# A Strassen-Winograd kernel: two quarter operands of a second-level step made as one full-width operand, and one more product split a second time

## The chip, the cores and the metric

One core of a Trainium2 chip runs one program. The metric is the device time in microseconds (us) of one execution; of several runs the median is given. TensorE (PE) multiplies, VectorE (DVE) and ScalarE (ACT) prepare operands and take results out of PSUM, GpSimd (POOL) and SyncE (SP) issue transfers.

## The reference, cut to what matters

```python
# x: 2048 x 1024, fp32; dft matrices 1024^2 and 2048^2; w1: 1024 x 3584; w2: 3584 x 1024
a, b = x @ hid_re.T, x @ hid_im.T                 # stage x
y = seq_re @ a - seq_im @ b                       # stage C ("sequence"), K = 4096
h = relu(x @ w1 + b1) ** 2                        # stage h: part 0 (2048 columns), part 1 (1536)
o = h @ w2 + b2                                   # stage o ("output"), K = 3584
g = sigmoid((x * gate_w).sum(-1, keepdims=True))
out = g * y + (1 - g) * o
```

All of it is fp32 and nearly all of the work is in four large matrix products.

## The kernel before, in words

Each number is split into a high and a low part that TensorE takes at its fast rate: `hi` is the value rounded by ScalarE (`ACTIVATE hi<-raw`), `lo` is what VectorE leaves over (`TENSOR_TENSOR lo<-raw,hi`). A product of two operands is then three matmuls: hi by hi, hi by lo, lo by hi (`Group.run`).

A stage is a Winograd variant of Strassen's scheme: seven products of half-size blocks in place of eight, with block sums S1 to S4 of the left side and T1 to T4 of the right (`FACTORS` says which product takes which block or sum). `seven` walks through the products in the order of a tuple (1, 2, 5, 6, 3, 7, 4). A product runs either whole (`direct`) or is split once more into seven (`twice`). Which are split stands in tables: `TWICE_X`, `TWICE_C`, `TWICE_O` and, for the two parts of stage h, `TWICE_H`. Before, part 0 of h splits all seven, part 1 splits all but product 7.

There are two shapes of stage. `wide` (stages x and h) has a short inner dimension. A whole product is 8 steps of `rows` * 6 matmuls, a split one 7 steps; `rows` is 4, and 3 in part 1 of h, so that a step there is 18 matmuls. In a split product the seven steps run in the order 5, 1, 3, 6, 2, 7, 4; steps 1, 6, 7 and 4 form a chain that goes on adding in the same PSUM tiles, which are read out behind every step, before the next step of the chain may write there. Steps 7 and 4 follow each other directly. `tall` (stages C and o) has a long inner dimension and splits for 2 * k of its blocks, k from the table; there the left operands of the second level are 256 wide. Such an operand has its high and its low part in one tile, `both`. Blocks (0,1) and (1,1) of the second level (steps 2 and 4) are the two 256-wide halves of one block `base[1, q]` of the first level, and before each of them is made as an operand of its own: two ACT instructions and two DVE instructions of 128x512.

The order of the work is not written down. The kernel records its operations, and `plan` lays them out: a list scheduler with due times counted back from an unbroken run of matmuls, 55 tile slots that are handed out in the order of need, and four PSUM tiles. `emit` then writes that one order, so every instruction of an engine has the same source line (L1512 in the profile) and groups are told apart by tile names: `raw` loaded, `sum` a block sum, `h`, `u`, `y`, `o` results, `ps` PSUM. Tables choose between equal ways of one thing: `MINUS` makes a low part by an ACT copy and an adding transfer of POOL in place of DVE; `LAND`, `LAND2` and `MADE` make block sums by adding transfers; `LOW` and `HIGH` keep finished low and high parts in HBM and fetch them again; `RELU` lets DVE do the bias and the relu of a quarter of h.

Of the kernel before, what the change touches and what calls it, by code (L numbers as in the profile page):

```python
# [22 lines left out]
FIRST_C, FIRST_O = {1: 6, 2: 5, 3: 5, 6: 3, 7: 6}, {6: 3, 7: 3}  # L23
# [2 lines left out]
LAND_X, LAND_C, LAND_H, LAND_O = {"T1": 4}, {"T1": 16, "T3": 4, "T4": 15}, ({"T1": 4, "T3": 2}, {"T3": 4}), {"T1": 8, "T3": 2, "T4": 11}
# [2 lines left out]
ADD_O = range(13)
GATE, ROWS = (-30, 2), (24, 24)  # L30
OLD_X, OLD_H = (2, 3, 4), ((3, 4, 2, 6), (3,))
# [1 line left out]
LOW, HIGH = ({1: 125, 2: 35, 3: 119, 4: 32, 5: 7, 6: 3, 7: 6}, {1: 4, 2: 125, 3: 119, 4: 1, 5: 127, 6: 112, 7: 1}), ({5: 64, 6: 8, 7: 65}, {2: 2, 3: 35, 4: 42, 6: 64, 7: 18})
# [1 line left out]
LAND2_X, LAND2_C, LAND2_H, LAND2_O = {}, {1: {"T3": 3}, 2: {"T1": 4, "T3": 3}, 3: {"T1": 3, "T3": 3}, 4: {"T1": 3, "T3": 1}, 6: {"T1": 1}, 7: {"T1": 1}}, ({2: ("T1",), 5: ("T1",), 3: ("T1", "T3"), 6: ("T3",)}, {1: ("T3",), 2: ("T3",), 5: ("T3",), 3: ("T3",)}), {1: {"T1": 1}, 2: {"T1": 3, "T3": 1}, 3: {"T1": 3, "T3": 3}, 4: {"T1": 2, "T3": 3}, 5: {"T1": 2, "T3": 1}, 6: {"T1": 1}}
MADE = {"T1": 2600, "T3": 12076}
TWICE_H = (1, 2, 5, 3, 4, 6, 7), (1, 2, 5, 3, 4, 6)
# [13 lines left out]
LATE, PATIENT = 60.0, (20.0, 0)  # L51
# [1511 lines left out]
```

## Time and profile before

| what | us |
|---|---|
| median of 3 runs | 1821.21 (1816.94, 1821.21, 1821.67) |
| the profiled execution | 1817.16 |
| its span, first to last instruction | 1815.4 |
| PE busy | 1799.3 (99%) |
| DVE busy | 1713.9 (94%) |
| ACT busy | 1172.8 (65%) |
| POOL busy | 279.3 (15%) |

The span is what the profiler saw of the program, and 1.8 us of the execution lie outside it. Matmuls overlap, so that a single one lasts 0.39 us while they start 0.23 us apart; times of matmuls are therefore read from their starts. By the count of matmuls the stages lie at about 6 to 283 us (x), to 836 (C), to 1103 (h part 0), to 1308 (h part 1) and to 1800 (o).

### The profile page before, as it was taken

The page shows a single profiled execution, that of the slowest core. Times are in us where ns is not written, and L with a number is a line of the kernel's source. Part 1 is how long each engine was busy: PE and PEld are TensorE (multiplying, and loading weights), DVE is VectorE, ACT ScalarE, POOL GpSimd, SP SyncE. Part 2 cuts the span into 40 slices and gives each one's busy share as a digit, 9 for nine tenths or more (in the row PEclk, how much of TensorE's full clock was granted, in tenths as well). Part 3 has the DMA queues.
Part 4 walks back from the last instruction along what each step waited for, and adds up shares of the span by engine and source line. Part 5 has one row for each costly group of instructions (what it writes and reads, how often), then busy time and mean ns, then how long its engine had stood idle before and what let it go on. Part 6 is the DMA issues. An engine that isn't in the chain of part 4 may idle for free. (4 is left out here: it accounts for less than half of the span.)

```text
span 1815.4 us, 22435 instructions
## 1 busy us (share of the span) xinstructions
PE 1799.3 (99%) x7940; PEld 1484.2 (82%) x7940; DVE 1713.9 (94%) x1758; ACT 1172.8 (65%) x1362; POOL 279.3 (15%) x408
## 2 busy tenths in 40 slices
PE   9999999999999999999999999999999999999998
PEld 7888888888888888888888888878788888888886
DVE  8999989999999999999888999688898999999997
ACT  6465655674666564667684749968986566675662
POOL 1202112011211000211210211012121021101121
PEclk9999999999999999999999999999999999999999
DMA  9999999899999689989998889999999999879986
GB/s 349 319 395 356 397 332 317 285 258 306 256 344 304 183 293 374 283 212 351 329 360 255 283 312 310 375 385 339 321 375 249 345 207 307 292 202 339 308 237 134
DMA packets 155872, 552.68 MB, mean 304 GB/s; under 512 B 17504, under 2 KB 17776, under 8 KB 155760
## 3 DMA queue, kind: packets, MB, share of 16 engines
q1 hardware_dynamic: 96768, 345.70, 50.9%
q0 software_dynamic: 58704, 205.16, 42.3%
q8 instruction: 62, 1.02, 0.2%
q10 hardware_dynamic: 288, 0.39, 0.1%
q14 instruction: 50, 0.41, 0.1%
HBM read 397.56 MB, written 138.42 MB: 295 GB/s over the span
## 5 line engine op out<-in xcount | busy, mean ns | idle before, releaser
L1512 PE MATMUL ps<-hi,both 128*128 128x512 f32 x2072 | 640.6, 389 | 0.8 <-ACT ps L1512 0.4
L1512 PE MATMUL ps<-hi 128*128 128x512 f32 x1596 | 621.4, 390 | 4.5 <-ACT hi L1512 2.3
L1512 PE MATMUL ps<-hi,lo 128*128 128x512 f32 x1596 | 620.7, 389 | 1.6 <-DVE lo L1512 1.6
L1512 PE MATMUL ps<-lo,hi 128*128 128x512 f32 x1596 | 620.5, 389 | 0.0
L1512 ACT ACTIVATE hi<-raw 128x1024 fp32r<-128x1024 f32 (+2 forms) x412 | 419.2, 1034 | 210.2 <-PE ps L1512 72.9
L1512 PEld LDWEIGHTS ps<-hi,both 128*128 128x128 f32 x2072 | 388.7, 188 | 82.9 <-ACT ps L1512 1.4
L1512 DVE TENSOR_TENSOR lo<-raw,hi 128x1024 fp32r<-128x1024 f32 (+2 forms) x353 | 414.8, 1189 | 30.8 <-ACT hi L1512 24.1
L1512 PE MATMUL ps<-lo,both 128*128 128x512 f32 x1036 | 403.5, 389 | 0.3 <-DMA lo<-sum 0.3
L1512 PEld LDWEIGHTS ps<-hi 128*128 128x128 f32 x1596 | 299.5, 188 | 70.2 <-ACT hi L1512 3.8
L1512 PEld LDWEIGHTS ps<-hi,lo 128*128 128x128 f32 x1596 | 299.6, 188 | 64.9 <-DVE lo L1512 2.4
L1512 PEld LDWEIGHTS ps<-lo,hi 128*128 128x128 f32 x1596 | 299.5, 188 | 62.2 <-DVE lo L1512 0.4
L1512 ACT ACTIVATE hi<-sum 128x1024 fp32r<-128x1024 f32 (+1 forms) x215 | 220.8, 1034 | 137.2 <-DVE sum L1512 95.8
L1512 DVE TENSOR_TENSOR lo<-sum,hi 128x1024 fp32r<-128x1024 f32 (+1 forms) x203 | 239.7, 1190 | 14.3 <-ACT hi L1512 11.1
L1512 PEld LDWEIGHTS ps<-lo,both 128*128 128x128 f32 x1036 | 194.5, 188 | 41.6 <-DMA lo<-sum 1.1
L1512 DVE TENSOR_TENSOR raw<-raw 128x1024 f32<-128x1024 f32 (+1 forms) x164 | 193.0, 1196 | 3.7 <-DMA raw<-in_w1b 1.3
L1512 DVE TENSOR_TENSOR sum<-raw 128x1024 f32<-128x1024 f32 (+2 forms) x181 | 177.4, 986 | 6.2 <-PE ps L1512 3.3
L1512 DVE TENSOR_TENSOR sum<-raw,sum 128x1024 f32<-128x1024 f32 (+2 forms) x138 | 144.9, 1050 | 2.8 <-PE ps L1512 2.5
L1512 ACT ACTIVATE both<-sum 128x512 fp32r<-128x512 f32 x148 | 90.7, 625 | 79.4 <-DVE sum L1512 74.5
L1512 ACT ACTIVATE u<-ps 128x1024 f32<-128x1024 f32 x104 | 101.6, 979 | 29.8 <-PE ps L1512 29.5
L1512 ACT ACTIVATE both<-raw 128x512 fp32r<-128x512 f32 x111 | 68.5, 623 | 53.6 <-PE ps L1512 13.5
L1512 DVE TENSOR_TENSOR both<-sum,both 128x512 fp32r<-128x512 f32 x148 | 99.7, 683 | 0.6 <-ACT both L1512 0.5
L1512 DVE TENSOR_TENSOR u<-u,ps 128x1024 f32<-128x1024 f32 x74 | 86.4, 1178 | 7.6 <-PE ps L1512 5.9
(80 smaller groups left out, 1092.1 us busy)
## 6 DMA issues: line engine op xcount, KB each, us to landing
raw<-in_ct SPq DMA_DIRECT2D x130, 512.0 KB, 7.2
raw<-h SPq DMA_DIRECT2D x99, 512.0 KB, 7.1
raw<-in_w SPq DMA_DIRECT2D x94, 512.0 KB, 9.1
raw<-copy SPq DMA_DIRECT2D x73, 512.0 KB, 7.2
raw<-ab SPq DMA_DIRECT2D x71, 512.0 KB, 8.4
raw<-in_x SPq DMA_DIRECT2D x51, 512.0 KB, 9.1
copy<-raw POOLq DMA_DIRECT2D x46, 512.0 KB, 8.1
lo<-lo SPq DMA_DIRECT2D x46, 512.0 KB, 7.4
```

The source lines that it names most:

```text
L1512: made = getattr(real[op.engine], op.name)(*(actual(a) for a in op.args), **{k: actual(v) for k, v in op.kwargs.items()})
```

## The change

Part 1 of h now splits product 7 too. In stages C and o the operands (0,1) and (1,1) of a split product are made at once, as one 512-wide operand with a tile `hi` and a tile `lo`, and steps 2 and 4 take a half each (`Half`). A class `Twin` would do the same for S1 and S3; it is switched by bit 0 of `TWINS`, which isn't set. `RELU` now gives DVE one quarter of part 1 of h. The other tables are set anew.

```diff
-FIRST_C, FIRST_O = {1: 6, 2: 5, 3: 5, 6: 3, 7: 6}, {6: 3, 7: 3}
+FIRST_C, FIRST_O = {1: 6, 2: 5, 6: 4, 7: 6}, {6: 3, 7: 3}
...
-ADD_O = range(13)
-GATE, ROWS = (-30, 2), (24, 24)
+ADD_O = range(8)
+GATE, ROWS = (-30, 2), (20, 20)
...
-TWICE_H = (1, 2, 5, 3, 4, 6, 7), (1, 2, 5, 3, 4, 6)
+TWICE_H = (1, 2, 5, 3, 4, 6, 7), (1, 2, 5, 3, 4, 6, 7)
...
-EARLY_C, EARLY_O = 0, 65535
+EARLY_C, EARLY_O = 65535, 65535
...
-MINUS_C, MINUS_O = {2: 133124, 3: 8388624, 4: 8388613, 5: 50331652, 6: 8519745}, {1: 16, 2: 8, 3: 267264, 4: 12591136, 5: 9221, 6: 5243142, 7: 6291464}
-RELU = (), ()
+MINUS_C, MINUS_O = {2: 133124, 3: 8425522, 4: 8912905, 5: 33554436, 6: 1179713, 7: 4096}, {1: 16, 2: 8390664, 3: 410628, 4: 12595208, 5: 9221, 6: 6, 7: 6422568}
+RELU = (), (0,)
+TWINS_C, TWINS_O = 2, 2
...
+                    if block.seen and block.home == "slot" and not op.load and not block.seen[0][0].load:
+                        op.after.add(block.seen[0][0])
...
             for q in range(k):
                 again = Sums(lambda j, c, q=q: right[2 * q + j, c].of(r), SUMS_R2, True)
                 again.made.update({key: r2[q].of(key) for key in ("T1", "T2")})
+                pair = Operand(base[1, q]) if twins & 2 else None
                 for p2 in (2, 4, 3):
                     l_, r_ = FACTORS[p2]
-                    own.append((l2[q].operand(l_, 256), subtracted(p, again.operand(r_)), groups[p2],
+                    own.append((Half(pair, 256 * (p2 == 4)) if pair and p2 != 3 else l2[q].operand(l_, 256), subtracted(p, again.operand(r_)), groups[p2],
                                 [(2 * q + j, c) for j in range(2) for c in range(2)] if p2 == 3 else ()))
```

`LAND`, `LAND2`, `MADE`, `LOW`, `HIGH`, `OLD_H` and `PATIENT` change in the same manner, in their numbers only.

Three places of the instruction order follow. The first is VectorE near the beginning of stage C, in the split of product 1. Before, block `raw_2504` gives two operands:

```order
L1512 TENSOR_TENSOR sum_2995<-raw_2910,sum_2604 128x1024
L1512 TENSOR_TENSOR lo_3002<-raw_2910,hi_2981 128x1024
L1512 TENSOR_TENSOR both_2989<-raw_2504,both_2989 128x2x256
L1512 TENSOR_TENSOR both_3008<-raw_2504,both_3008 128x2x256
L1512 TENSOR_TENSOR lo_3026<-sum_2995,hi_3012 128x1024
L1512 TENSOR_TENSOR lo_3035<-raw_2644,hi_3022 128x1024
```

Now the same block, `raw_2507`, gives one:

```order
L1542 TENSOR_TENSOR sum_2996<-raw_2914,sum_2605 128x1024
L1542 TENSOR_TENSOR lo_3003<-raw_2914,hi_2981 128x1024
L1542 TENSOR_TENSOR lo_3014<-raw_2507,hi_2991 128x1024
L1542 TENSOR_TENSOR lo_3025<-sum_2996,hi_3007 128x1024
L1542 TENSOR_TENSOR lo_3034<-raw_2651,hi_3017 128x1024
```

The pair of 128x512 has become a single 128x1024, and the rows around it keep their order. ACT changes in the same way.

The second place is VectorE in product 7 of part 1 of h. Before, the results of a group, in two PSUM tiles, are added to `h` as the group ends, between operands that it makes:

```order
L1512 TENSOR_TENSOR h_10236<-h_10236,ps_10857 128x1024
L1512 TENSOR_TENSOR h_10269<-h_10269,ps_10874 128x512
L1512 TENSOR_TENSOR lo_11031<-sum_10985,hi_10998 128x2x384
L1512 TENSOR_TENSOR lo_11039<-raw_10923,hi_11027 128x1024
L1512 TENSOR_TENSOR h_10409<-h_10409,ps_10937 128x1024
L1512 TENSOR_TENSOR lo_11064<-raw_10849,hi_11046 128x2x384
L1512 TENSOR_TENSOR h_10425<-h_10425,ps_10952 128x512
```

Now they are added to `u`, behind every step:

```order
L1542 TENSOR_TENSOR u_10494<-u_10494,ps_10899 128x1024
L1542 TENSOR_TENSOR u_10506<-u_10506,ps_10924 128x512
L1542 TENSOR_TENSOR lo_11025<-sum_10992,hi_11002 128x2x384
L1542 TENSOR_TENSOR sum_11030<-raw_10793,sum_10913 128x768
L1542 TENSOR_TENSOR u_10494<-u_10494,ps_10939 128x1024
L1542 TENSOR_TENSOR u_10506<-u_10506,ps_10969 128x512
L1542 TENSOR_TENSOR raw_10941<-raw_10941,raw_10136 128x768
L1542 TENSOR_TENSOR lo_11060<-sum_11030,hi_11044 128x2x384
```

The read-outs of PSUM stand closer together, and `u` is added to `h` later.

The third place is PE in the same product, with the semaphores that an instruction waits for. Before, a group of product 7 starts in a PSUM tile that the group ahead of it does not use:

```order
L1512 MATMUL ps_10874<-hi_10867,hi_10879 128x512
L1512 MATMUL ps_10874<-lo_10882,hi_10879 128x512
L1512 MATMUL ps_10874<-hi_10867,lo_10897 128x512
L1512 MATMUL ps_10937<-hi_10885,hi_10822 128x512 [waits Activation_49]
L1512 MATMUL ps_10937<-lo_10909,hi_10822 128x512
```

Now, at the border from step 7 to step 4 of the split product, the tile is one that the step before has written, and that VectorE has to read first:

```order
L1542 MATMUL ps_10969<-lo_11000,hi_11002 128x512
L1542 MATMUL ps_10969<-hi_10984,lo_11025 128x512
L1542 MATMUL ps_10939<-hi_11034,hi_11044 128x512 [waits DVE_49,Activation_49]
L1542 MATMUL ps_10939<-lo_10954,hi_11044 128x512 [waits DMAHW4_49]
L1542 MATMUL ps_10939<-hi_11034,lo_11060 128x512
```

The first matmul of step 4 now waits for a DVE read of `ps_10939` that stands, in the DVE rows above, four rows ahead of the last low part of that step.

## Rows read from the trace of the kernel before

**Rows 1.** The page: the span, and the engines' busy time, share and instructions.

```profile
span 1815.4 us, 22435 instructions
PE 1799.3 (99%) x7940; PEld 1484.2 (82%) x7940; DVE 1713.9 (94%) x1758; ACT 1172.8 (65%) x1362; POOL 279.3 (15%) x408
```

**Rows 2.** Timeline of PE at both ends: start, duration, instruction, [idle before <-releaser].

```profile
5.96 0.73 PE L1512 MATMUL ps<-hi 128*128 128x512 f32 x2 [0.99 <-ACT hi L1512]
...
1807.14 0.39 PE L1512 MATMUL ps<-hi,lo 128*128 128x512 f32 x1
```

**Rows 3.** Groups by shape, PE, warm-up: count | busy us, mean ns | idle before.

```profile
L1512 PE MATMUL ps<-ones 128*128 128x128 bf16 x44 | 3.9, 274 | 1.1 <-DVE ones L1512 1.1
```

**Rows 4.** The chain that ended last: start, length, what, its longest piece.

```profile
1633.15 171.67 PE ps L1512 x756
```

**Rows 5.** PE's waits over the whole span: total us, times, longest.

```profile
PE ps L1512 <- ACT hi L1512: 2.3, 2, 1.3
PE ps L1512 <- DVE lo L1512: 1.6, 1, 1.6
...
PE ps L1512 <- ACT ps L1512: 0.4, 1, 0.4
```

**Rows 6.** Timeline of PE in part 1 of h, at the borders of split products.

```profile
1132.63 0.50 PE L1512 MATMUL ps<-hi 128*128 128x512 f32 x1 [0.52 <-DVE u L1512]
...
1161.12 0.39 PE L1512 MATMUL ps<-hi,lo 128*128 128x512 f32 x1
1161.55 0.47 PE L1512 MATMUL ps<-hi 128*128 128x512 f32 x1
...
1191.71 0.50 PE L1512 MATMUL ps<-hi 128*128 128x512 f32 x1 [1.27 <-DVE h L1512]
...
1249.49 0.47 PE L1512 MATMUL ps<-hi 128*128 128x512 f32 x1
...
1312.28 0.47 PE L1512 MATMUL ps<-hi 128*128 128x512 f32 x1 [1.32 <-ACT hi L1512]
```

**Rows 7.** Stretches C, h part 1, o: us, busy us (count) by engine, clock, DMA.

```profile
283.00:836.00 553.00, 552.66 (x2434) 456.21 (x2433) 544.08 (x581) 344.11 (x406) 72.31 (x93) 1.00 0.93 289
...
1103.00:1308.00 205.00, 203.08 (x891) 166.57 (x890) 169.16 (x182) 177.88 (x233) 31.95 (x51) 1.00 1.00 354
1308.00:1800.00 492.00, 489.99 (x2160) 404.83 (x2159) 479.21 (x514) 316.11 (x369) 72.54 (x90) 1.00 0.92 277
```

**Rows 8.** Groups by shape, DVE, ACT and POOL: the operations that the change touches.

```profile
L1512 ACT ACTIVATE hi<-raw 128x1024 fp32r<-128x1024 f32 x382 | 397.6, 1054 | 198.2 <-DVE raw L1512 67.0 <-PE ps L1512 66.7 <-DMA raw<-copy 10.3
L1512 DVE TENSOR_TENSOR lo<-raw,hi 128x1024 fp32r<-128x1024 f32 x323 | 388.6, 1217 | 16.8 <-ACT hi L1512 10.4 <-PE ps L1512 3.1 <-ACT h L1512 2.8
L1512 DVE TENSOR_TENSOR u<-u,ps 128x1024 f32<-128x1024 f32 x69 | 83.1, 1215 | 7.6 <-PE ps L1512 5.9 <-ACT u L1512 0.8
L1512 DVE TENSOR_TENSOR both<-raw,both 128x512 fp32r<-128x512 f32 x111 | 74.3, 682 | 0.0
L1512 ACT ACTIVATE both<-raw 128x512 fp32r<-128x512 f32 x111 | 68.5, 623 | 53.6 <-PE ps L1512 13.5 <-DVE raw L1512 12.8 <-DMA raw<-in_w 8.2
L1512 ACT ACTIVATE h<-h,b1c 128x512 f32<-128x512 f32 x97 | 65.5, 711 | 2.0 <-DVE h L1512 2.0
L1512 DVE TENSOR_TENSOR lo<-sum,hi 128x768 fp32r<-128x768 f32 x21 | 20.0, 953 | 10.5 <-ACT hi L1512 7.7 <-PE ps L1512 2.8
L1512 DVE TENSOR_SCALAR g<-g 128x1024 f32<-128x1024 f32 x2 | 1.3, 682 | 0.0
```

**Rows 9.** DMA totals in h part 1, then in its stretch 1140 to 1170.

```profile
DMA packets 21171, 72.48 MB, mean 354 GB/s; under 512 B 2385, under 2 KB 2385, under 8 KB 21158
...
DMA packets 3461, 11.83 MB, mean 394 GB/s; under 512 B 388, under 2 KB 388, under 8 KB 3457
```

**Rows 10.** The chain ahead of the matmul at 1191.71: start, length, what.

```profile
1177.91 7.27 issue
1185.20 5.32 DMA h<-h
```

More of the change, by code (lines that the diff above doesn't have):

```diff
@@ L22 @@
 TWICE_X, TWICE_C, TWICE_O = (1, 2, 5, 3, 4), {1: 4, 2: 4, 3: 4, 4: 4, 5: 3, 6: 1, 7: 1}, {1: 2, 2: 3, 3: 3, 4: 3, 5: 3, 6: 1, 7: 1}
[L23 removed]
+FIRST_C, FIRST_O = {1: 6, 2: 5, 6: 4, 7: 6}, {6: 3, 7: 3}
 WARM = 44
 FAR_TALL, FAR_WIDE = ("T2",), ()
[L26 removed]
+LAND_X, LAND_C, LAND_H, LAND_O = {"T1": 4}, {"T1": 16, "T3": 2, "T4": 15}, ({"T3": 2}, {"T3": 3}), {"T1": 9, "T3": 4, "T4": 11}
 SHARE = ("S1", "S2", "S3", "S4")
 NEAR_O = ("T1",)
[L29 to L31 removed]
+ADD_O = range(8)
+GATE, ROWS = (-30, 2), (20, 20)
+OLD_X, OLD_H = (2, 3, 4), ((3, 4, 2), (3, 6))
 SHARE2 = {1: 15, 2: 15, 3: 15, 4: 15, 5: 15, 6: 15, 7: 15}
[L33 removed]
+LOW, HIGH = ({1: 125, 2: 35, 3: 119, 4: 32, 5: 7, 6: 113, 7: 19}, {1: 4, 2: 125, 3: 127, 4: 1, 5: 127, 6: 112, 7: 9}), ({1: 1, 2: 32, 5: 64, 6: 8, 7: 73}, {3: 19, 4: 42, 6: 64, 7: 18})
 SPILL, LAND_CL = (8, 0), {"S1": 1}
[L35 to L37 removed]
+LAND2_X, LAND2_C, LAND2_H, LAND2_O = {3: ("T1",), 4: ("T1", "T3"), 5: ("T3",)}, {1: {"T3": 3}, 2: {"T1": 4, "T3": 3}, 3: {"T1": 3, "T3": 2}, 4: {"T1": 2}, 6: {"T1": 1}, 7: {"T1": 1}}, ({1: ("T1", "T3"), 2: ("T1",), 5: ("T1", "T3"), 3: ("T1", "T3"), 4: ("T3",), 6: ("T3",)}, {1: ("T3",), 2: ("T3",), 5: ("T3",), 3: ("T1",), 7: ("T3",)}), {1: {"T1": 1}, 2: {"T1": 3, "T3": 1}, 3: {"T1": 3, "T3": 3}, 4: {"T1": 1, "T3": 3}, 5: {"T1": 2, "T3": 1}, 7: {"T1": 1}}
+MADE = {"T1": 3112, "T3": 3628}
+TWICE_H = (1, 2, 5, 3, 4, 6, 7), (1, 2, 5, 3, 4, 6, 7)
 MM, MM_END, FIRST_MM = 0.2267, 0.18, 6.2
@@ L47 @@
 APART_C, APART_O = (0, 0), (0, 0)
[L48 to L49 removed]
+MINUS_C, MINUS_O = {2: 133124, 3: 8425522, 4: 8912905, 5: 33554436, 6: 1179713, 7: 4096}, {1: 16, 2: 8390664, 3: 410628, 4: 12595208, 5: 9221, 6: 6, 7: 6422568}
+RELU = (), (0,)
+TWINS_C, TWINS_O = 2, 2
 BEGIN, OUT, NOT_OUT = 1, 15, ((1, 1, 0, 1), (1, 1, 1, 1))
[L51 removed]
+LATE, PATIENT = 60.0, (30.0, 0)
 LEAD = {"raw": 11.5, "hi": 6.0, "sum": 5.0, "out": -0.1}
@@ L282, in __init__ @@
             super().__init__("part")
-            self.lands = lands
+            self.lands, self.twin = lands, None
             self.blocks, self.op, self.width, self.copy = ([a] if b is None else [a, b]), op, width, None
@@ L314, in make_parts @@
             mine = [t for t in self.slots if t is not None]
-            self.slot, self.done = mine[0] if mine else take("sum", width=self.width), True
+            self.slot, self.done = mine[0] if mine else self.twin() if self.twin else take("sum", width=self.width), True
             for k, c in self.cuts:
@@ L337, in rest, with __init__, half, load @@
             pass
+    class Twin(Near):
+        def __init__(self, a, b):
+            super().__init__("twin")
+            self.blocks, self.whole = [a, b], None
+            a.twin, b.twin = (lambda: self.half(0)), (lambda: self.half(256))
+            a.uses += 1
+            b.uses += 1
+        def half(self, at):
+            self.whole = self.whole or take("sum")
+            return self.whole[:, :, at:at + 256]
+        def load(self, engines):
+            pass
+        def sum(self):
+            self.slot, self.done = self.whole, True
+        def rest(self):
+            for b in self.blocks:
+                b.used()
     class Onto(Near):
@@ L690, in tall @@
              sums=SUMS_L, lands_l={}, less=LESS, early=0,
-             now=(0, 0, 0), apart=(0, 0), minus={}):
+             now=(0, 0, 0), apart=(0, 0), minus={}, twins=0):
         left = {q: Sums(lambda i, j, q=q: left_(i, j, q), sums, far=FAR_TALL, lands=spread(lands_l, q, ksteps))
@@ L866, in twice @@
             for q in range(k):
+                if twins & 1:
+                    pair = Operand(Twin(l2[q].of("S1", 256), l2[q].of("S3", 256)))
                 for p2 in (1, 6, 7, 5):
                     l_, r_ = FACTORS[p2]
-                    step(l2[q].operand(l_, 256), subtracted(p, r2[q].operand(r_)), groups[p2])
+                    step(Half(pair, 256 * (p2 == 7)) if twins & 1 and p2 in (5, 7) else l2[q].operand(l_, 256), subtracted(p, r2[q].operand(r_)), groups[p2])
             def to(m, c):
@@ L1204, in c_stage @@
         tall(lambda i, j, q: ab[j, q, i], lambda j, n, q, c: ct[n, c, j, q], 8, TALL_C, TWICE_C, FIRST_C, target, final,
-             lands=LAND_C, lands2=LAND2_C, sums=SUMS_LC, lands_l=LAND_CL, less=LESS_C, early=EARLY_C, now=NOW_C, apart=APART_C, minus=MINUS_C)
+             lands=LAND_C, lands2=LAND2_C, sums=SUMS_LC, lands_l=LAND_CL, less=LESS_C, early=EARLY_C, now=NOW_C, apart=APART_C, minus=MINUS_C, twins=TWINS_C)
         return at, rows
@@ L1265, in o_stage @@
         tall(lambda i, j, q: w2[i, j, q], lambda j, n, q, c: h_far[j, q, 2 * (1 - n) + c], 7, TALL_O, TWICE_O, FIRST_O,
-             target, final, last, LAND_O, sums_far, LAND2_O, early=EARLY_O, now=NOW_O, apart=APART_O, minus=MINUS_O)
+             target, final, last, LAND_O, sums_far, LAND2_O, early=EARLY_O, now=NOW_O, apart=APART_O, minus=MINUS_O, twins=TWINS_O)
         return at, rows
@@ L1301, in ready @@
         o = o.base if isinstance(o, (View, Half)) else o
-        if id(o) in made or not isinstance(o, (Part, Onto, Operand, Fetched, Gate, Row)):
+        if id(o) in made or not isinstance(o, (Part, Onto, Twin, Operand, Fetched, Gate, Row)):
             return
```

## Prediction

> **What bounds the kernel now.** I read the page first, for shares: PE is busy 1799.3 of 1815.4 us, DVE 1713.9 [rows 1]. A busy PE says little, since matmuls overlap, so next the ends of its timeline and the longest piece of the chain. The first real matmul starts at 5.96, the last at 1807.14 [rows 2]; the page's 7940 matmuls less 44 of warm-up [rows 3] are 7896. In the longest unbroken piece 756 of them take 171.67 us [rows 4], that is 0.2271 us from start to start. At that pace 7895 starts take 1793.0 us, and from first to last there are 1801.2. So only 8.2 us of the whole program are waits of PE. Some 6 us come ahead of the first matmul, about 8 behind the last start, and the rest is matmuls at full pace. The bound is the number of matmuls; every other engine counts only where PE waits for it.
>
> Where PE waits is told by its list of waits, and by the timeline around each. The largest single one, 1.6 us for a `lo` of DVE, is at the start of the program [rows 5]. Most of the others lie in part 1 of h, at one kind of place: 1132.63, 1161.55, 1191.71, 1249.49 and 1312.28, with 1220.60 like 1161.55 [rows 6]. These are the borders between step 7 and step 4 of the six split products, where DVE must read a PSUM tile before PE goes on in it. With three row blocks the first tile is complete only six matmuls, 1.36 us, before step 4 begins, and the read is 1.2 us long [rows 8]. So every such border costs something. A bracketed idle counts from the modelled end of a matmul that lasts 0.39 us at a pace of 0.23, so 0.16 is added: 0.68, 1.43 and 1.48 us for the three long ones. The three short ones start 0.43 us after their predecessor, 0.20 too late. Together 4.19 us, 0.70 each: half of all waiting.
>
> **The change part by part.** *Product 7 of part 1.* Whole, it is 8 steps of 18 matmuls, 144; split, 7 steps, 126. Eighteen matmuls less at 0.2271 us [rows 4] are **-4.09 us**, all on the path, since PE is the path. Against that it makes a seventh border of steps 7 and 4, which the PE rows of the order show with its wait for DVE. The six rows bound its price from 0.20 to 1.48 us; I take their mean, **+0.70** [rows 6], since long and short are equally many. Below nothing is excluded: the tile is read at the same distance as at the other six.
>
> What else the split adds lies beside PE. By the instruction lists for the matmuls of part 1, DVE gets six more `u<-u,ps` of each size (1.215 us, the half-size ones 0.68 as other two-input work of 128x512 [rows 8]), 11.4 us; it loses four full and five half adds of PSUM to `h`, -8.3; it gets eight more sums and low parts 768 wide at 0.953 [rows 8], +7.6; six other operations less, -6.2. The relu of a quarter, 12 instructions of 128x512, moves there from ACT. Its price on DVE is bounded by the one-input row of 128x1024, 0.682 us [rows 8], and by half of it, 0.34; nearer the half, as the size is, I take 0.4 and get 4.8. Sum: +9.3 us on 169 [rows 7], so 178.5 of 201 us, 89%. ACT loses 12 times 0.711 [rows 8], 8.5 us, in the part where several stretches had it full; that is cover gained. Were DVE's cover gone, the borders above would be the first to lengthen, up to 1.48 each, and that is in the second rival.
>
> A rule of the Trainium skill speaks against the moved relu. What the rows show first: DVE takes 0.682 us for 1024 elements of one input, 1.217 for two inputs [rows 8]. The Trainium skill, in SBUF — State Buffer, Who interferes with whom, says that a `tensor_scalar` in its two-port mode holds a port pair that GpSimd shares, and that transfers issued from GpSimd wait meanwhile. By it the sum would be up to 4.8 us higher, as the third rival works out; without it, as above.
>
> *Twins in C and o.* 37 pairs (21 in C, 16 in o, the sums of the tables) lose 74 `both` and gain 37 full-width parts. DVE: 74 times 0.682 less, 37 times 1.217 more, -5.4 us. ACT: 74 times 0.623 less, 37 times 1.054 more, -7.1 us [rows 8]. PE runs the same number of matmuls there. DVE is busy 544 of 553 us in C and 479 of 492 in o [rows 7], yet PE, counted from its busy times [rows 7], loses only 0.3 us in C and 2.0 in o, of which 1.3 are the border at 1312.28. So this buys slack and no time: **0**, with a lower end of -1.7 (four waits of 0.2 to 0.4 us in x, C and o, of which the last row of [rows 5] is the longest, each with 0.16 added). Above: a pair holds its two tiles until step 4 is done, and the first use of it waits for both halves; the price would be a longer wait at the start of a split product, bounded by the longest wait for an operand in the trace, 1.6 [rows 5].
>
> *The tables.* `EARLY` is read by whole products alone, and C has none; the entry of `FIRST_C` for product 3 is unused, since its split takes all blocks; `ADD_O` counts results that all go another way. All three do nothing. `MINUS` moves nine low parts more from DVE to an ACT copy and an adding transfer: 11 us off DVE, 9.5 onto ACT, nine more transfers on POOL. With it all lists hold 19 more transfers of half a megabyte, four of them within part 1. SP passes no late load for them, since SP only issues; POOL is busy 15% [rows 1]. **0** on the path; upper end in the second rival.
>
> *The new order.* Any new plan of the same work shifts waits by some tenths. I take 0; the likeliest bounds are those of the two first rivals.
>
> **Sum:** -4.09 + 0.70 = **-3.4 us**. The profiled execution took 1817.16 us, the three runs 1816.94, 1821.21 and 1821.67; it is 4.05 below their median, and the mean of the four is 1819.2. Since executions of this kernel differ by nearly 5 us, I set the sum against that mean: **1815.8 us** (1813.8 against the profiled one).
>
> **The rivals.** *A: faster by more.* With the relu off ACT and `both` pairs gone, the three long borders become short ones: 0.20 in place of 0.68, 1.43 and 1.48 saves 3.0, and the seventh is short too. Then -4.09 + 0.20 - 3.0 = -6.9, or **1812.3**; with the -1.7 of C and o it is -8.6, or 1810.6. For it: the border at 1312.28 waits for ACT [rows 6], which gets freer. Against it: that at 1191.71 hangs on a store of `h`, which the chain follows back through 7.27 us without an instruction and 5.32 us of transfer [rows 10]; nothing in the change makes stores sooner.
>
> *B: slower, transfers in part 1.* Part 1 moves 72.5 MB in 205 us, 354 GB/s [rows 9], with the DMA engines always busy [rows 7]. The four added transfers of up to 0.5 MB make about 74.4 MB, and 201 us are left: 370 GB/s. If 354 is all it can do, the part takes 210.2 us, +5.2 against 205: **1824.4**, slower than before. It decides as soon as the sustained rate is below 363 GB/s, where 74.4 MB take the 205 us of now. For it: stores release a border [rows 10]. Against it: in a stretch of 30 us inside the same part 394 GB/s flowed [rows 9]. The Trainium skill, in HBM Reference, Specifications (TRN2), gives about 358 GB/s as a core's share and about 425 for a core that streams alone; by the first figure part 1 would take an estimated 208 us, by the second it has room, and the 394 here agrees with the second.
>
> *C: the relu on DVE delays POOL.* Each one-input instruction of DVE holds up an issue of POOL by at most its 0.68 us [rows 8], and if each of seven borders hangs on a store, as one does now [rows 10], 7 times 0.68 is +4.8, or **1820.6** with the sum, 1.4 above now. Against it: POOL is idle 85% of the time [rows 1], and twelve instructions are few.
>
> That the change does nothing can be left out: the lists have 7878 matmuls in place of 7896.
>
> **How the numbers follow.** Forecast 0.55, A 0.24, B 0.15, C 0.06. A measurement of this kernel can tell about 0.3%, 5.5 us, from no change. The forecast is 3.4 us and so within; but runs spread by 4.7, so 0.11 of its 0.55 go to faster. A is beyond 5.5 us but for 0.02. B lies just at the bound: 0.08 of it count as slower, and 0.02 of C. So faster 0.33, same 0.57, slower 0.10. The range goes from A's far end, 1810.6, to B, 1824.4.
>
> **What would show it.** In the new profile: 7922 matmuls on the page with the warm-up; the stretch of part 1 shorter by 3 to 4 us; PE's timeline with seven late starts there, 0.2 to 1.5 us each; 37 `both<-raw` on ACT and on DVE in place of 111; DVE at some 95%. Rival A would show as waits of PE shorter in sum by 3 us or more, B as DMA at full share in part 1 with PE waiting behind loads or stores, C as gaps of POOL that end on a `TENSOR_SCALAR`. I am wrong if PE's waits from first to last matmul grow beyond 14 us, or if new ones appear in C or o, where the pair is made.

## The result, and the profile after

The changed kernel takes 1821.4 us, the median of 22 runs, and the kernel before 1818.8, of as many on the same chips. The ratio is 1.0015, interval 1.0009 to 1.0021: slower by 2.6 us by the medians and 2.7 by the ratio, where 3.4 less was forecast. That lies within the range and within 0.3%, but on the other side of no change. The two profiled executions differ a little more: 1821.70 against 1817.16 us.

The page of the kernel after:

```profile
span 1819.9 us, 22430 instructions
...
PE 1799.6 (99%) x7922; PEld 1480.6 (81%) x7922; DVE 1727.9 (95%) x1748; ACT 1155.6 (63%) x1308; POOL 281.9 (15%) x412
```

The 18 matmuls are gone, 7922 for 7940 [rows 1], and the span is still 4.5 us longer. So PE waits more. The windows by stage say where, in the same stretches as before (us, busy us and count by engine, clock, DMA share, GB/s):

```profile
core 0: us, PE busy (x) PEld busy (x) DVE busy (x) ACT busy (x) POOL busy (x), PEclk, DMA share, GB/s
6.00:283.00 277.00, 275.16 (x1206) 225.88 (x1207) 268.44 (x259) 160.26 (x165) 58.85 (x101) 1.00 0.99 360
283.00:836.00 553.00, 550.98 (x2423) 453.66 (x2422) 539.34 (x555) 342.60 (x387) 74.78 (x96) 1.00 0.95 291
836.00:1103.00 267.00, 266.03 (x1172) 219.47 (x1171) 245.84 (x216) 163.74 (x181) 40.03 (x67) 1.00 0.91 317
1103.00:1308.00 205.00, 202.07 (x884) 165.13 (x883) 181.17 (x203) 154.47 (x195) 27.45 (x45) 1.00 0.99 362
1308.00:1800.00 492.00, 488.68 (x2149) 402.34 (x2148) 484.14 (x505) 331.47 (x381) 77.49 (x96) 1.00 0.96 286
```

Read the count behind PE: how many matmuls went through in that time. Before it was 1208, 2434, 1178, 891 and 2160. Now it is 2, 11, 6, 7 and 11 fewer, 37 in all, and 37 times 0.227 us is 8.4 us. Take off the 18 matmuls that are gone, 4.1 us, and add 0.2 at the two ends: that is the 4.5 us of the span. Most of the loss of this execution lies in C and o. PE's list of waits:

```profile
engine line waited for: us in total, times, longest us
PE ps L1542 <- DVE h L1542: 3.1, 6, 1.0
PE ps L1542 <- ACT ps L1542: 2.4, 3, 1.3
PE ps L1542 <- DVE both L1542: 2.0, 3, 0.8
...
PE ps L1542 <- DVE u L1542: 0.9, 2, 0.5
PE ps L1542 <- DVE ab L1542: 0.7, 1, 0.7
```

Against [rows 5] no single long wait has come in, but many small ones, for what DVE makes (`h`, `both`, `u`, `ab`) or for what ACT makes right behind DVE (`ps`). Three of PE's late starts from the timeline: a new one in C, the new border of steps 7 and 4 in product 7, and the longest wait of stage o:

```profile
480.79 0.73 PE L1542 MATMUL ps<-hi,both 128*128 128x512 f32 x2 [0.61 <-DVE both L1542]
...
1283.24 0.39 PE L1542 MATMUL ps<-hi,lo 128*128 128x512 f32 x1
1283.93 0.47 PE L1542 MATMUL ps<-hi 128*128 128x512 f32 x1 [0.31 <-ACT hi L1542]
...
1714.61 0.39 PE L1542 MATMUL ps<-hi,lo 128*128 128x512 f32 x1
1716.25 0.50 PE L1542 MATMUL ps<-hi 128*128 128x512 f32 x1 [1.25 <-ACT ps L1542]
```

The border costs 1283.93 - 1283.24 less the pace of 0.23, or 0.47 us. The one in stage o costs 1.42. DVE's timeline ahead of it, and ACT's row behind that:

```profile
1707.70 1.22 DVE L1542 TENSOR_TENSOR lo<-raw,hi 128x1024 fp32r<-128x1024 f32 x1
1708.84 1.21 DVE L1542 TENSOR_TENSOR u<-u,ps 128x1024 f32<-128x1024 f32 x1
1710.08 1.23 DVE L1542 TENSOR_TENSOR u<-u 128x1024 f32<-128x1024 f32 x1
1711.41 1.22 DVE L1542 TENSOR_TENSOR u<-u,ps 128x1024 f32<-128x1024 f32 x1
1712.67 1.23 DVE L1542 TENSOR_TENSOR u<-u 128x1024 f32<-128x1024 f32 x1
1713.81 2.34 DVE L1542 TENSOR_TENSOR u<-u,ps 128x1024 f32<-128x1024 f32 x2
...
1715.19 1.95 ACT L1542 ACTIVATE ps<-u 128x1024 f32<-128x1024 f32 x2
```

DVE runs one instruction behind the other. The sum that must go back into PSUM, the first of the last two, is done at 1715.03; from 1715.19 ACT copies it there in 1.01 us, and only then may PE go on. The stretches ahead of three late starts of stage o (1346.00, 1572.92 and 1716.25), in the windows of the kernel before:

```profile
1680.00:1716.00 36.00, 36.00 (x160) 29.83 (x159) 35.60 (x35) 22.33 (x25) 4.65 (x5) 1.00 1.03 314
1540.00:1573.00 33.00, 33.00 (x148) 27.32 (x147) 32.69 (x34) 21.60 (x26) 2.12 (x4) 1.00 0.89 329
1315.00:1346.00 31.00, 31.00 (x139) 25.66 (x138) 30.96 (x36) 29.89 (x40) 8.85 (x15) 1.00 0.98 342
```

and after:

```profile
1315.00:1346.00 31.00, 30.37 (x134) 24.78 (x133) 30.90 (x36) 29.46 (x38) 7.11 (x11) 1.00 0.92 291
1540.00:1573.00 33.00, 32.16 (x143) 26.32 (x141) 32.72 (x34) 19.54 (x22) 2.00 (x4) 1.00 0.81 293
1680.00:1716.00 36.00, 35.00 (x155) 28.65 (x153) 35.79 (x36) 21.87 (x24) 7.41 (x7) 1.00 1.05 306
```

DVE is full in both, 30.9 of 31 us, and yet PE waited nowhere before. A full DVE is thus not by itself a wait. It becomes one where the one result that PE needs next stands late in DVE's queue, as in the rows above. That led to the theories below.

### The profile page after: what moved, and what is told of

Same layout as the page of the kernel before. It is cut to its first block, busy times and chain, and to the rows that moved or that the text cites. A ratio compares the mean times of both kernels' runs of the same rounds, so it can differ in the third digit from the quotient of the medians.

```text
span 1819.9 us, 22430 instructions
## 1 busy us (share of the span) xinstructions
PE 1799.6 (99%) x7922; PEld 1480.6 (81%) x7922; DVE 1727.9 (95%) x1748; ACT 1155.6 (63%) x1308; POOL 281.9 (15%) x412
## 5 line engine op out<-in xcount | busy, mean ns | idle before, releaser
L1542 PE MATMUL ps<-hi 128*128 128x512 f32 x1886 | 735.4, 390 | 8.1 <-DVE h L1542 3.1
L1542 PE MATMUL ps<-hi,lo 128*128 128x512 f32 x1886 | 733.3, 389 | 0.7 <-DVE lo L1542 0.7
L1542 PE MATMUL ps<-lo,hi 128*128 128x512 f32 x1886 | 733.1, 389 | 0.0
L1542 PE MATMUL ps<-hi,both 128*128 128x512 f32 x1480 | 464.7, 390 | 2.1 <-DVE both L1542 2.0
L1542 PEld LDWEIGHTS ps<-hi 128*128 128x128 f32 x1886 | 354.1, 188 | 89.2 <-ACT ps L1542 4.4
L1542 PEld LDWEIGHTS ps<-lo,hi 128*128 128x128 f32 x1886 | 354.0, 188 | 72.7 <-DVE lo L1542 0.2
L1542 PEld LDWEIGHTS ps<-hi,both 128*128 128x128 f32 x1480 | 277.2, 188 | 62.4 <-DVE both L1542 4.6
L1542 PE MATMUL ps<-lo,both 128*128 128x512 f32 x740 | 288.2, 389 | 0.2
L1542 PEld LDWEIGHTS ps<-lo,both 128*128 128x128 f32 x740 | 138.9, 188 | 29.9 <-DVE lo L1542 1.0
L1542 ACT ACTIVATE ps<-u 128x1024 f32<-128x1024 f32 (+1 forms) x60 | 60.5, 1011 | 28.2 <-DVE u L1542 14.2
```

The source lines that it names most:

```text
L1542: made = getattr(real[op.engine], op.name)(*(actual(a) for a in op.args), **{k: actual(v) for k, v in op.kwargs.items()})
```

## The experiments

Four theories were set against each other. **1**: the pairs of C and o cost it. **2**: the new order of the work costs it, whatever the edit, since before's order was an unusually good one. **3**: the split pushes work of h into o. **4**: DVE's load; with less to do it would bring the late results in time. All runs in one table. The waits are those of the profiled execution: from the first to the last start of a stage, less its matmuls times 0.22675 us, about the pace of the stretches without a late start ("start" is the first 30 matmuls). At this pace before waits 11.0 us in all, at the 0.2271 of [rows 4] 8.2. They come from one execution each, and executions of one kernel differ by some us (before 1816.2 to 1821.7, after 1818.2 to 1825.9), so that 1 or 2 us in one stage prove little.

| kernel | us | ratio to before, interval | start | x | C | h 0 | h 1 | o | sum |
|---|---|---|---|---|---|---|---|---|---|
| before | 1818.8 | 1 | 2.3 | 1.0 | 1.4 | 0.3 | 4.9 | 1.1 | 11.0 |
| after | 1821.4 | 1.0015 (1.0009 to 1.0021) | 1.4 | 2.3 | 4.1 | 1.6 | 5.7 | 4.2 | 19.4 |
| split alone (e1) | 1825.3 | 1.0044 (1.0030 to 1.0058) | 1.4 | 2.5 | 1.9 | 0.0 | 4.5 | 12.3 | 22.5 |
| pairs alone (e2) | 1824.4 | 1.0037 (1.0025 to 1.0049) | 2.3 | 1.4 | 2.9 | 4.1 | 7.3 | 2.2 | 20.2 |
| no pairs (e3) | 1819.9 | 1.0007 (0.9998 to 1.0016) | 1.7 | 1.2 | 3.9 | 1.1 | 6.4 | 3.5 | 17.8 |
| no split (e4) | 1823.4 | 1.0035 (1.0022 to 1.0048) | 2.1 | 1.7 | 2.0 | 1.1 | 6.1 | 3.3 | 16.4 |
| no relu on DVE (e5) | 1823.3 | 1.0028 (1.0017 to 1.0039) | 1.8 | 1.4 | 2.7 | 1.8 | 10.3 | 6.7 | 24.7 |
| old tables of o (e7) | 1828.2 | 1.0049 (1.0037 to 1.0061) | 2.1 | 1.3 | 2.2 | 1.0 | 8.0 | 11.4 | 26.0 |
| before, lead of raw (n1) | 1818.8 | 0.9998 (0.9989 to 1.0006) | 1.8 | 1.5 | 1.1 | 2.2 | 4.8 | 1.9 | 13.2 |
| before, lead of hi (n3) | 1821.6 | 1.0016 (1.0007 to 1.0025) | 2.7 | 1.1 | 2.3 | 0.5 | 6.6 | 1.7 | 14.9 |
| after, lead of raw (m1) | 1819.6 | 1.0006 (0.9997 to 1.0014) | 2.0 | 1.4 | 2.3 | 0.8 | 7.1 | 4.0 | 17.6 |
| after, lead of hi (m3) | 1826.1 | 1.0040 (1.0028 to 1.0052) | 2.0 | 1.4 | 6.6 | 1.0 | 7.7 | 6.2 | 24.9 |
| after, DVE lighter (d1) | 1814.1 | 0.9975 (0.9966 to 0.9983) | 1.6 | 1.2 | 0.9 | -0.1 | 7.0 | 1.5 | 12.1 |
| before, DVE heavier (d2) | 1820.0 | 1.0008 (1.0000 to 1.0017) | 2.5 | 2.1 | 1.3 | 1.1 | 5.2 | 1.9 | 14.1 |
| after, DVE's end 0.60 (r1) | 1824.5 | 1.0027 (1.0017 to 1.0037) | 1.5 | 1.1 | 10.0 | 1.0 | 11.7 | 1.2 | 26.5 |
| after, DVE's end 0.50 (r2) | 1820.6 | 1.0005 (0.9997 to 1.0014) | 2.3 | 0.9 | 5.9 | 1.5 | 7.0 | 0.8 | 18.4 |
| r1, pairs in o alone (r3) | 1822.1 | 1.0019 (1.0010 to 1.0029) | 2.3 | 1.3 | 4.6 | 2.4 | 8.4 | 1.3 | 20.3 |
| before, DVE's end 0.60 (n4) | 1828.7 | 1.0048 (1.0034 to 1.0061) | 2.2 | 1.8 | 9.5 | 3.9 | 5.8 | 1.2 | 24.3 |
| after, low parts on POOL (f1) | 1845.6 | 1.0151 (1.0133 to 1.0170) | 2.0 | 1.3 | 15.8 | 4.9 | 6.9 | 9.5 | 40.5 |
| before, low parts on POOL (f2) | 1847.1 | 1.0166 (1.0146 to 1.0186) | 1.9 | 3.6 | 6.5 | 1.6 | 4.9 | 16.4 | 34.8 |

### The parts apart

**e1**, the kernel before with the split alone:

```diff
-TWICE_H = (1, 2, 5, 3, 4, 6, 7), (1, 2, 5, 3, 4, 6)
+TWICE_H = (1, 2, 5, 3, 4, 6, 7), (1, 2, 5, 3, 4, 6, 7)
```

> The kernel before with product 7 of h's second part split and nothing else changed: no pairs, old tables. Theory 1 (the pairs of C and o cost what was lost): 18 matmuls less and one border more, ratio about 0.998 (-3.4 us), waits of PE in C and o as before (about 3 us together). Theory 2 (any new plan away from the numbers that the tables of before were set for adds waits): 4 to 8 us more of waits spread over the stages, ratio 1.000 to 1.002. Theory 3 (the split itself pushes work of h into stage o): the waits of x and C stay, those of o grow by about 3 us, ratio 0.999 to 1.000.

**e2**, the code of the change with every table of before, and the pairs on (`TWINS_C, TWINS_O = 2, 2`):

> The kernel before with the full-width pairs in C and o and nothing else changed: product 7 whole, old tables. Theory 1 (pairs): PE waits of C and o grow from about 3 us to 7 or 8, ratio 1.002 to 1.003. Theory 2 (new plan): also 4 to 8 us more, but in every stage, x and h too, ratio 1.002 to 1.004. Theory 3 (split): nothing, ratio 0.999 to 1.001.

**e3**, the changed kernel without the pairs:

```diff
-TWINS_C, TWINS_O = 2, 2
+TWINS_C, TWINS_O = 0, 0
```

> The changed kernel with each quarter operand made by itself again, as before; split and new tables stay. Theory 1 (pairs): the 4 to 5 us that PE's waits in C and o grew by go away, ratio to before about 0.999. Theory 2 (new plan): no better than the changed kernel, 1.001 to 1.004. Theory 3 (split): as the changed kernel, 1.001 to 1.002.

**e4**, the changed kernel with product 7 of part 1 whole, by the line of e1 the other way round:

> The changed kernel with product 7 of h's second part whole again: 18 matmuls more, pairs and new tables stay. Theory 1 (pairs): the 4.1 us come back less one border, ratio to before about 1.003. Theory 2 (new plan): 1.002 to 1.005, the waits in any stage. Theory 3 (split): the waits in o fall back by about 3 us and the 18 matmuls cost 4.1, ratio about 1.002.

Taken alone into the old tables, either edit costs, by the ratios: the split 8.0 us, the pairs 6.7. Look where the waits of e2 arise: in h, where no pair is made, they go from 0.3 to 4.1 us in part 0 and from 4.9 to 7.3 in part 1. Theory 1 doesn't foresee that; a new order can do it. Without the pairs (e3) the changed kernel is 1.5 us faster (0.8 thousandths, the intervals overlap), at 1.0007 no better than before, and C keeps 3.9 of its 4.1 us of waits. So the pairs cost at most a part of what was lost. Theory 3 fits e1, with 12.3 us in o, but not e4, where o waits 3.3 us without the split, nor the changed kernel, where 4.2 come with it. In the changed tables the split does bring something: without it (e4) the time is 2.0 us longer by the medians and 3.6 by the ratios. The 18 matmuls less the new border, 4.09 - 0.47, would be 3.6. But e4 is a new order as well, with waits of its own (3.0 us fewer in the profiled execution, where only 0.5 are the border), so that this isn't the price of the split by itself.

### The same work in another order

`LEAD` is how many us before its use the planner lets a step begin. A tenth more changes no instruction and only the order. **n1** and **n3** on the kernel before, **m1** and **m3** on the changed one, `raw` 11.5 to 11.6 and `hi` 6.0 to 6.1:

```diff
-LEAD = {"raw": 11.5, "hi": 6.0, "sum": 5.0, "out": -0.1}
+LEAD = {"raw": 11.6, "hi": 6.0, "sum": 5.0, "out": -0.1}
```

> The kernel before, every operation and table kept, with one lead time of the plan moved by a tenth of a us (raw, 11.5 to 11.6): the same work on every engine in a slightly other order on DVE, ACT and POOL. Theory 2 (the plan of before is a chosen one, and any neighbour has more waits): PE's waits rise from 11 to 15 to 22 us, ratio 1.002 to 1.006. Theories 1 and 3 (pairs or split cost the time): nothing happens, ratio 0.9995 to 1.0005 or a scatter to both sides of it.

> As the run before it, with another lead time (hi, 6.0 to 6.1). Theory 2: ratio 1.002 to 1.006, waits in stages where nothing changed. Theories 1 and 3: 0.9995 to 1.0005 or a scatter to both sides.

> The changed kernel with the same step (raw, 11.5 to 11.6). If theory 2 holds and the plan of the changed kernel is an ordinary one, its neighbours scatter around it, ratio to before 0.999 to 1.003; if it is a chosen one as well, they are slower, 1.003 to 1.007. Theories 1 and 3: as the changed kernel, 1.0010 to 1.0020.

> The changed kernel with the other step (hi, 6.0 to 6.1). As for the run before it: 0.999 to 1.003 if the plan of the changed kernel is an ordinary one, 1.003 to 1.007 if it is a chosen one, 1.0010 to 1.0020 by theories 1 and 3.

The traces of all four hold the same instructions as their kernel, each as often. Around the kernel before one neighbour is equal and one 3 us slower; around the changed one they are 1.6 us faster (the intervals overlap) and 4.6 slower. So orders of identical work differ by as much as the whole forecast, and none of before's neighbours beats it. The step "I take 0" was thus a choice without a ground.

**e5**, the changed kernel with the relu of that quarter back on ACT (`RELU = (), ()`), and **e7** with before's `LAND`, `LAND2`, `MADE` and `MINUS` for stage o:

> The changed kernel with the relu of the quarter of h's second part on ACT again; the plan is made anew. The relu's share of DVE is 12 times 0.4 us. Theory 4: about 5 us less on DVE in h's second part and the beginning of o, 2 us less waiting there, ratio 1.000 to 1.001. Theory 2: a neighbour of the changed kernel's plan like the others, 1.0005 to 1.004. The third rival of the prediction (the relu on DVE holds up POOL): 1.4 to 4.8 us less, ratio 0.999 to 1.001.

> The changed kernel with stage o's tables of before (LAND_O, LAND2_O, MINUS_O and MADE); split, pairs and all other tables stay. If the new tables of o are what makes PE wait there (4 us in place of 1), the waits of o fall to 1 to 2 us, ratio 0.999 to 1.000. Theory 2 (any plan but the chosen one): waits of o 3 to 8 us, ratio 1.001 to 1.005. Theory 4: as many DVE instructions as MINUS_O gives, within 3 us of DVE, so nothing much, 1.001 to 1.002.

Neither gains. With the relu on ACT, h part 1 waits 10.3 us for 5.7, and with the old tables o waits 11.4 for 4.2. Both are new orders as well, so they don't price the relu or a table by itself; they show only that taking either back doesn't make the changed kernel faster.

### The load of DVE, in an unchanged order

**d1** keeps the changed kernel's order instruction by instruction, and every 20th low part is made by an instruction of one input. It leaves the values of 29 low parts out: they are zero.

```diff
...
+        low = op.engine == "vector" and op.name == "tensor_tensor" and op.outs[0].base.name == "lo"
...
+        if low and lows[0] % 20 == 0:
+            made = real["vector"].tensor_scalar(actual(op.args[0]), actual(op.args[2]), 0.0, 0.0, op0=ALU.mult,
+                                                op1=ALU.add)
...
```

> The changed kernel in its own order, where every 20th low part that DVE makes is set to zero by a one-input instruction in place of the subtraction (that low part is left out of the result): some 29 instructions, each about 0.5 us shorter, take about 14 us off DVE, the amount that the change put onto it. Theory 4 (the waits of PE are DVE's backlog, and the change made DVE fuller): PE's waits fall from 19 us to 11 to 13, ratio to before 0.997 to 0.9985. Theory 2 (the waits belong to the plan's order, whatever DVE's load): 17 to 20 us of waits, ratio 1.000 to 1.0015.

**d2** keeps before's order, and DVE clears a spare tile after every 20th of its instructions:

```diff
...
+            if lows[0] % 20 == 0:
+                tc.nc.vector.memset(spare, 0.0)
```

> The kernel before in its own order, with a small memset on DVE behind every 20th DVE instruction, nearly 90 in all, 0.1 to 0.2 us each, which nobody waits for: 9 to 17 us more on DVE, spread evenly. Theory 4 (DVE's load): PE's waits rise from 11 to 16 to 20 us, ratio 1.003 to 1.005. Theory 2: 11 to 13 us, ratio 1.000 to 1.001.

What d1 puts in place of 1.22 us each, by the groups by shape:

```profile
L1546 DVE TENSOR_SCALAR lo<-hi 128x1024 fp32r<-128x1024 f32 x26 | 17.9, 688 | 0.2 <-PE ps L1549 0.2
...
L1546 DVE TENSOR_SCALAR lo<-hi 128x768 fp32r<-128x768 f32 x3 | 1.7, 558 | 6.2 <-ACT hi L1549 6.2
```

and its windows of C, h part 1 and o:

```profile
283.00:836.00 553.00, 552.96 (x2436) 456.70 (x2436) 537.80 (x559) 344.06 (x387) 74.83 (x96) 1.00 0.94 293
...
1103.00:1308.00 205.00, 200.65 (x878) 163.99 (x877) 179.06 (x203) 152.94 (x193) 27.31 (x44) 1.00 1.00 360
1308.00:1800.00 492.00, 490.51 (x2161) 405.24 (x2160) 478.36 (x505) 327.49 (x376) 77.88 (x96) 1.00 0.94 284
```

These are 13 more matmuls in C than after and 12 more in o. With some 15 us less of DVE's work, under 1% of it, the time falls by 7.3 us, to 1814.1, below both kernels and below the forecast. DVE is then busy 1714.7 us, where before has 1713.9 and after 1727.9. In the profiled execution all of the gain comes from the stages outside part 1 of h; the borders of part 1, which hang on the distance of six matmuls, gain nothing. The instruction put in also doesn't read `raw`, so what the 0.5 us bring and what the missing operand brings isn't told apart.

In before's order 87 memsets of 165 ns, 14.4 us, cost 1.5 us by the ratio, where theory 4 alone asked for 5 to 9. So in the changed order the last 15 us of DVE's load turn places into waits, and before's order takes nearly as much more at little cost. Load alone isn't it either: in C DVE is busy 4.7 us less than before (539.34 for 544.08 [rows 7]), and PE waits 2.7 us more. Neither before with a lighter DVE nor after with a heavier one was run.

### A plan with more room, and less work for DVE in full

If close hand-offs (a matmul that needs a result made only a few matmuls earlier) are the fault, a planner that takes DVE for slower should make fewer of them. `VEC_END` is the time it allows from the end of a DVE instruction to its first use; **r1** sets 0.60 in place of 0.39, **r2** 0.50, **r3** 0.60 with the pairs in o alone, and **n4** 0.60 in the kernel before:

```diff
-VEC, VEC_END, ACT, ACT_END = (0.07, 1.0417e-3), 0.39, (0.09, 0.843e-3, 0.04, 0.095), 0.41
+VEC, VEC_END, ACT, ACT_END = (0.07, 1.0417e-3), 0.6, (0.09, 0.843e-3, 0.04, 0.095), 0.41
```

> The changed kernel, its tables and every operation kept, with a plan that takes DVE's results to arrive 0.60 us after an instruction in place of 0.39, so that it lays DVE's work earlier. In the order of the instructions 24 results of ACT or DVE (or reads of PSUM) are followed by the matmul that needs them within 4 matmuls, against 31 in the changed kernel and 20 in the one before. Theory 2 (the order decides, at the same work): waits of PE 11 to 15 us in place of 19, ratio 0.9975 to 0.9995. Theory 4 alone (DVE's load decides): nothing changes, 1.001 to 1.002.

> As the run before it with 0.50 us; 23 such places. Theory 2: ratio 0.9975 to 0.9995. Theory 4 alone: 1.001 to 1.002.

> As the first of these, with pairs in stage o alone; 21 such places, the fewest. Theory 2: ratio 0.997 to 0.999. Theory 1 (the pairs cost the time): the waits of C alone fall, to 1.5 us. Theory 4 alone: 1.001 to 1.002, since DVE gets 3 us more.

> The kernel before with 0.60 us: 28 such places in place of 20. Theory 2: waits rise from 11 to 14 to 17 us, ratio 1.001 to 1.003. Theory 4 alone: 0.9995 to 1.0005, since the work is the same.

This failed. The waits of o do go, from 4.2 to between 0.8 and 1.3 us, but C gets 4.6 to 10.0 in their place; r2 ends a thousandth better than the changed kernel, r1 a thousandth worse, r3 within half a thousandth, and before's own work loses 10 us by the medians, 8.7 by the ratio. Counted in the programs' own order, matmuls that come within four of their operand number 20 in before and 31 in after, 24, 23 and 21 in r1 to r3 and 28 in n4; the times don't follow. So in these six counting close hand-offs didn't tell a good order.

**f1** and **f2** take the load off DVE and leave nothing out: low parts whose first matmul is at least 50 matmuls away, no two of them closer than 120, are subtracted by POOL, in the changed kernel's order (43 of them) and in before's (47).

```diff
...
+            first = min(op.then, key=lambda o: at[id(o)])
+            if first.engine == "tensor" and at[id(first)] - at[id(op)] >= 50 and at[id(op)] >= free:
+                op.engine, free = "gpsimd", at[id(op)] + 120
```

> The whole work, in the changed kernel's own order, with 43 low parts (raw minus hi, 128x1024) done by POOL in place of DVE: those whose first matmul comes at least 50 matmuls later, and no two of them closer than 120. That takes some 50 us off DVE and moves nothing else. Theory 4 (DVE's load): the waits outside part 1 of h go, as they did with 14 us less, so 1812 to 1816 us, 0.995 to 0.998, waits of PE 11 to 13 us. Theory 2 (the order alone): the order is the same, so 1.001 within 0.001. Rival: POOL takes several times as long as DVE for one, and the transfers that it issues come late behind it, so new waits of PE on loads, over 1825 us.

> The same in the kernel before and its own order: low parts with at least 50 matmuls to spare, no two closer than 120, go from DVE to POOL. Theory 4: before has little to win, since 14 us more on DVE cost it 1.5 us: 0.997 to 1.0, and by the 18 matmuls it stays behind the changed kernel with the same edit. Theory 2: 1.0 within 0.001. Rival: POOL's transfers come late, over 1822 us.

The page of f1, and its groups by shape:

```profile
PE 1804.7 (98%) x7922; PEld 1481.8 (80%) x7922; DVE 1740.4 (95%) x1705; ACT 1154.8 (63%) x1308; POOL 435.8 (24%) x455
```

```profile
L1551 DVE TENSOR_TENSOR lo<-raw,hi 128x1024 fp32r<-128x1024 f32 x325 | 401.2, 1253 | 16.1 <-ACT hi L1551 11.7 <-ACT u L1551 2.9 <-issue 1.1
L1551 POOL TENSOR_TENSOR lo<-raw,hi 128x1024 fp32r<-128x1024 f32 x27 | 94.6, 3502 | 128.2 <-ACT hi L1551 69.0 <-PE ps L1551 35.3 <-DVE lo L1551 14.3
L1551 POOL TENSOR_TENSOR lo<-sum,hi 128x1024 fp32r<-128x1024 f32 x13 | 55.5, 4266 | 27.2 <-ACT hi L1551 25.6 <-PE ps L1551 1.6
```

The time is the rival's, over 1825 us, but not for its reason: in PE's list no wait ends on a load; the longest entries are ACT's `ps`, 9.7 us, and DVE's `lo`, 6.2. DVE has 43 instructions less than after and is busy 12.5 us longer, so that theory 4 wasn't tested: the load didn't fall. The last section tells why. Whether an order of the changed work, with all of it done, reaches the forecast stays open; of its orders tried the best were r2 and m1, 1.0005 and 1.0006, and none that does all the work beats before.

## Why the prediction was right or wrong

**The 18 matmuls: right.** They are gone, at 0.227 us each, and putting them back (e4, in an order of its own) costs 2.0 to 3.6 us. The pace was taken a little too long, since the 171.67 us of [rows 4] run to the end of the last matmul: by the starts it is about 0.2267, and before waits some 11 us and not 8.2.

**The seventh border: right in its bounds.** It costs 0.47 us, between the bounds of 0.20 and 1.48, though in this execution it ends on ACT's `hi` and not on the read of PSUM. The seven cost 0.19, 1.15, 0.72, 0.64, 0.38, 0.47 and 0.74, in sum 4.3, and the six of before 4.2 [rows 6]. Part 1 of h waits 5.7 us for 4.9 in all; that this +0.8 is so near the forecast +0.70 is luck, since the borders together gave only 0.1 of it.

**Rival A: wrong.** The long borders did become shorter, 1.15 at most for 1.48, but the short ones longer, and the sum stood still.

**Rival B: wrong.** In the stretch of part 1 362 GB/s flowed, more than the 354 of [rows 9], at a DMA share of 0.99. That is no more than the 363 at which the rival was to decide, but the waits decide against it: no wait of PE there ends on a transfer, and from its first matmul to that of stage o part 1 takes 205.7 us for 209.0. The range ended at this rival's time, and the measured time lies inside it for another reason: luck.

**Rival C: wrong.** The relu on DVE takes 0.48 us, in the bounds of 0.34 and 0.68:

```profile
L1542 DVE TENSOR_TENSOR both<-raw,both 128x512 fp32r<-128x512 f32 x37 | 25.2, 681 | 0.0
L1542 ACT ACTIVATE both<-raw 128x512 fp32r<-128x512 f32 x37 | 23.1, 625 | 32.6 <-DVE raw L1542 22.6 <-DMA copy<-sum 7.8 <-DMA raw<-in_w 1.3
L1542 DVE TENSOR_SCALAR h<-h,b1c 128x512 f32<-128x512 f32 x12 | 5.2, 479 | 0.0
```

The twelve run between 1157.34 and 1174.45, and POOL runs nothing from 1150.2 to 1171.0; its two issues of 1171.02 fall between two of them. So no issue of POOL was held up by one, and whether a relu can hold one up no run here shows. Nor is the time shorter without the relu on DVE (e5). The 37 pairs stand there as counted, too.

**The failed step: "*The new order.* Any new plan of the same work shifts waits by some tenths. I take 0".** Outside part 1 of h the waits grew from 6.1 to 13.6 us, 7.5 in the profiled executions: x +1.3, C +2.7, h part 0 +1.3, o +3.1, the start -0.9. By the ratio 2.7 - (-3.4) = 6.1 us were lost against the forecast. How far an order alone can go, n1 to m3 show: orders of identical work lie 0 to 4.6 us from their neighbour, and n4 about 9. Of the three neighbours of before none was faster, and with 11.0 us of waits in 1818.8 there was little to win. The term was not 0 with a width of tenths, but a loss of some us.

**What the step rested on: "So this buys slack and no time: 0", "0 on the path" for DVE's work.** I read that PE lost 0.3 us in C (1.4 by the starts) while DVE was busy 544 of 553 [rows 7] as proof that DVE didn't matter there. It proves only that in that one order each late result was placed early enough. d1 shows what the load is worth once the order isn't so lucky: 15 us of DVE for 7.3 us of time.

**The sum for DVE was wrong as well.** The entries -5.4, +9.3 and -11 make 7.1 us less for DVE; the pages show 14.0 more, 1727.9 for 1713.9 [rows 1]. The pairs and `MINUS` came out as counted. But the list for the split held only what runs during part 1: eight adds `h<-h,u` of the split product, 7.6 us, run in stage o, between 1360.8 and 1388.3, and some of the operations counted as saved only moved there. So the split does push work of DVE into o, as theory 3 has it, but between 1346.34 and 1485.19 no matmul starts more than 0.1 us late, so that no wait is seen for it at that place. In part 0 of h, where only tables changed, DVE is busy 2.6 us more (245.84 for 243.21 in its stretch).

The prediction named the sign of its own failure: waits beyond 14 us from first to last. At its pace of 0.2271 they are 16.6, and new or longer ones stand in C (480.79, and 323.92 with 0.94 us for 0.35 at 322.90 before, both for `both`) and in o (1346.00, 1572.92, 1716.25). Not settled is what makes one order better than another, and how much of the 6.1 us belongs to the order and how much to the 14 us more on DVE: with some 15 us of DVE's work gone (d1) all of it came back, but 29 low parts were left out.

## What to carry to other kernels

Where the bound engine is 99% busy and the next one 95%, a change that makes a planner lay all the work out anew has a term of its own. Here it was a loss, and the likely reason is that the old plan was a chosen one. Measure its size beforehand, by a planner constant that changes no instruction, and set a gain of a few tenths of a per cent against that scatter. And a saving that is exact on paper should be weighed in the changed plan (take the part out of the whole) and not only added to the old one: the same split cost 8 us in the old tables and gave 2 to 4 in the new, each time in another order.
